# Attention and feed-forward on one core: order of the steps that share a PSUM bank, and the score banks of the first batch's last tiles

## The chip, the cores and the metric

The kernel runs on one core of one Trainium2 chip. The metric is the device time of one execution in microseconds, the median over several runs. TensorE (PE in the views, PEld for its weight loads) multiplies, VectorE (DVE), ScalarE (ACT) and GpSimd (POOL) do the rest, SyncE (SP) issues the transfers.

## The reference

```python
scores = scale * np.matmul(q, k.transpose(0, 1, 3, 2))       # 8 x 8 heads, 576 x 64
thresh = np.max(scores, axis=-1, keepdims=True) - tau
scores = np.where(scores >= thresh, scores, -1000000000.0)
scores = scores - np.max(scores, axis=-1, keepdims=True)
attn = np.exp(scores)
attn = attn / (np.sum(attn, axis=-1, keepdims=True) + 1e-09)
x = np.matmul(attn, v)               # heads joined: 4608 x 512
h = x @ w_in                         # 512 x 2048
r = np.maximum(h, 0.0)
g = s * (r * r) + b
out = g @ w_out                      # 2048 x 512
```

## The kernel before

Attention goes by tiles of 128 queries of one head. The first batch has 36 tiles (`n_plain` = 36), computed with fp32 products (`plain_tile`): scores on TensorE into a PSUM bank, row maximum on DVE (line 529), threshold on POOL (531), exponential on ACT (533), mask and sum on DVE (535), reciprocal (538, 540), scaling on POOL (541), transposes on TensorE (549), copy on ACT (553), products with v (562), copy-out (566). The other seven batches (`split_tile`) work with pairs of fp16 pieces, and their attention is transposed by DMA.

The feed-forward takes blocks of 256 rows. Each has a stage (scaled fp16 pieces of x, lines 806 to 828) and 16 steps: 24 products into bank `h`, relu, square and cast on ACT (847, 850, 851), a remainder (852), and 24 products into the double bank `o`. At the end, line 871 scales `o` and adds a row that comes from `b`. Three pairs of buffers `gs` (tiles `gh`, `gl`) pass from the h products to the o products.

The weights arrive in 16 parts (f = 0 to 15) and are decoded (lines 670, 673, 665). `weight_sizes(k)` for four parts at a time takes products into bank `h` and their maximum (688, 692). `sums(k)` adds the columns of four parts of w_out: eight product records into bank `h` (768), copied (772) or added (774) into `part`; after k = 3 a product with `both` spreads the sum over the partitions (777) and ACT multiplies it with `b` (778). `bias` later copies it to its place (781). `weight_scales` reduces the maxima (698), turns them with a product into bank `h` (701), reduces (702), spreads (706) and makes the power `wpower` (707 to 715). `pieces_of_weights(f)` needs `wpower` and splits every part in two fp16 pieces, first on ACT (737), then on DVE (741).

`keep_busy` adds filler products (983) without use for the result. All steps are added to a plan with engine, cost, what they read and write, and a due time. The order in which they are added decides which of two steps that write the same buffer or bank comes first. `Plan.run` then lists the steps of each engine by a cost model, and `NUDGES` shifts the due time of chosen steps (kind, number, how many, by how many ns) before the last listing. The order of events is that of the number in front of each. Tiles with i < `TWO_BANKS` use score bank `s` or `o` in turn, later plain tiles all use `s`.

Of the kernel before, what the change touches and what calls it, by code (L numbers as in the profile page):

```python
# [23 lines left out]


NUDGES = (
# [35 lines left out]
)  # L62


# [2 lines left out]
LEAST, UP, DOWN = 2.0 ** -120, 2.0 ** -52, 2.0 ** 51  # L67
H_DOWN = 2.0 ** -21
BUSY, BUSY_TILES, BUSY_EACH = 16, 12, 5
TWO_BANKS = 30  # L70
WEIGHTS_AT, WEIGHTS_EACH = 12, 1.5
STACKS_IN = (None, 0, 7, 8, 9, 10, 11, 12)
VALUES_IN = (1, 2, 3, 4, 5, 6)
SPARES = (2, 3, 1, 5, 6, 4)


# [119 lines left out]
def tile_attention_ffn(ctx: ExitStack, tc: tile.TileContext, qT, kT, v, tau, w_in, w_out, s, b, out):  # L196
# [65 lines left out]
    def spare(f):  # L262

        return lazy["whole", SPARES[f], 0]

# [19 lines left out]
    def split_buffers():  # L285
# [9 lines left out]
        for n, f in enumerate(STACKS_IN):  # L295
# [4 lines left out]
            claim([f"y{n}"] + (old_ if f is None else [(f"w{f}", "o")]) + [("y", n, c) for c in range(2)], y)  # L300
        for n, f in enumerate(VALUES_IN):
            def y(n=n, f=f):
# [477 lines left out]
    def bias(at):  # L780
        act((465, 565), lambda: nc.scalar.copy(out=spare(2), in_=part),
            ["part", (f"w{SPARES[2]}", "i", 2)], ["bias"] + [f"g{n}{i}" for n in "hl" for i in range(3)], at)

# [182 lines left out]
    n_plain = sum(vis[0] == 0 for vis in visits) // 2 * 9  # L966
# [46 lines left out]
    events = []  # L1013
# [15 lines left out]
    for f in range(NF):  # L1029
        events.append((WEIGHTS_EACH * f, lambda f=f: (load_weights(f, 2 + f), weights(f, 2 + WEIGHTS_EACH * f))))  # L1030
        if f % 4 == 3:
            events.append((WEIGHTS_EACH * f + 0.1, lambda f=f: (weight_sizes(f // 4, 2.5 + WEIGHTS_EACH * f), sums(f // 4, 2.5 + WEIGHTS_EACH * f))))
    events.append((n_plain - 0.6, lambda: weight_scales(WEIGHTS_AT)))
    for f in range(NF):
        events.append((n_plain - 0.5, lambda f=f: convert(f)))
    events.append((n_plain - 0.4, lambda: bias(WEIGHTS_AT + 2)))
    step, when = 0, 0.0
    for i, ti in enumerate(tiles):
        ti.tag = "o" if i < TWO_BANKS and i % 2 else "s"

# [68 lines left out]
```

## Time and profile before

| | us |
|---|---|
| median of 3 runs | 1121.05 |
| lowest, highest | 1116.58, 1124.85 |
| profiled execution, its own time | 1119.29 |
| span of the profiled execution | 1117.4 |
| PE busy | 1093.1 |
| ACT busy | 965.8 |
| DVE busy | 914.1 |
| POOL busy | 541.0 |

The profile holds one execution. Busy time is the time in which at least one instruction of an engine is under way; for TensorE, products overlap and their ends are modelled. The granted TensorE clock is 0.998 of full speed.

### The profile page before, as it was taken

The numbers are of one execution on the slowest core, as the hardware profiler recorded it, in microseconds if no ns is written. First come the engines' busy times: TensorE is split into PE (matmuls) and PEld (weight loads), VectorE is DVE, ScalarE is ACT, GpSimd is POOL, SyncE is SP. The second block draws the span as 40 slices with busy tenths as digits, with TensorE's granted clock in tenths as the row PEclk, the third lists the DMA queues.
The fourth block names the chain that finished last, engine by engine and source line by source line (L and its number), as shares of the span: only waits on it lengthen the run. The fifth ranks groups of instructions, "written<-read, shape, count | busy, mean of one in ns | idle before, by whom it ended". The sixth has DMA issues, their size and how long they took to land.

```text
span 1117.4 us, 38384 instructions
## 1 busy us (share of the span) xinstructions
PE 1093.1 (98%) x15026; PEld 948.0 (85%) x15026; DVE 914.1 (82%) x1947; ACT 965.8 (86%) x2293; POOL 541.0 (48%) x1113
## 2 busy tenths in 40 slices
PE   9999999999999999999999999999999999999998
PEld 7776777878788999888999998888888988888876
DVE  6897888999899999989988899988989888884021
ACT  8996988899899989999988899989989989995443
POOL 6645554455446445555544455545535455553200
PEclk9999999999999999999999999999999999999999
DMA  9920079879986998879876789868887976472000
GB/s 286 393 95 1 14 163 198 123 149 170 185 158 122 186 190 169 150 141 186 175 133 104 145 153 184 150 120 174 149 147 144 173 134 146 89 127 45 10 21 21
DMA packets 359078, 157.05 MB, mean 141 GB/s; under 512 B 313328, under 2 KB 340464, under 8 KB 358896
## 3 DMA queue, kind: packets, MB, share of 16 engines
q1 hardware_dynamic: 358896, 154.60, 69.5%
q8 instruction: 118, 1.93, 0.7%
q14 instruction: 64, 0.52, 0.1%
HBM read 46.01 MB, written 9.44 MB: 50 GB/s over the span
## 4 chain that ended last, share of the span: by engine, by line
PE 74%; ACT 8%; DMA 7%; DVE 7%; issue 3%; POOL 0%; SPq 0%; DVEq 0%; ACTq 0%; POOLq 0%
PE h L277 26%; PE o L277 26%; PE pv L626 7%; DMA eb<-en 4%; PE t L277 4%; PE s L277 3%; DMA ea<-en 2%; ACT en L608 2%; PE s L526 2%; PE pv L562 2%; PE t L549 1%; DVE em L602 1%; ACT em L600 1%; PE o L526 1%; DVE st L594 1%
## 5 line engine op out<-in xcount | busy, mean ns | idle before, releaser
L277 PE MATMUL h<-xp,iw 128*64 128x256 f16 x6912 | 438.5, 273 | 6.9 <-ACT iw L847 6.7
L277 PEld LDWEIGHTS <-iw 128*64 128x64 f16 x6912 | 399.1, 110 | 32.0 <-issue 11.2
L277 PEld LDWEIGHTS <-gs 128*64 128x64 f16 x3456 | 251.0, 110 | 67.8 <-POOL gs L852 1.6
L852 POOL TENSOR_TENSOR gs<-iw,gs 128x256 f16<-128x256 f32 x272 | 198.1, 729 | 198.9 <-ACT gs L851 92.4
L277 PE MATMUL o<-ow,gs 128*64 128x512 f16 x1944 | 251.9, 380 | 0.5 <-POOL gs L852 0.5
L611 DVE SCALAR_TENSOR_TENSOR en<-em,st,en 128x576 f16<-128x576 f32 x252 | 208.6, 830 | 20.8 <-ACT en L608 19.0
L608 ACT ACTIVATE en<-em,st 128x576 f16<-128x576 f32 x252 | 193.5, 770 | 18.3 <-DMA eb<-en 7.6
L277 PE MATMUL o<-iw,gs 128*64 128x512 f16 x1512 | 195.7, 379 | 0.2 <-DVE iw L871 0.2
L596 POOL TENSOR_SCALAR st<-st,wz 128x1 f32<-128x1 f32 x252 | 122.8, 488 | 109.5 <-DVE st L594 67.2
L847 ACT ACTIVATE iw<-h 128x256 f32<-128x256 f32 x288 | 108.9, 378 | 66.6 <-PE h L277 63.0
L605 POOL TENSOR_SCALAR st<-st 128x1 f32<-128x1 f32 x252 | 88.1, 350 | 137.5 <-DVE em L602 71.9
L850 ACT ACTIVATE iw<-iw 128x256 f32<-128x256 f32 x288 | 120.0, 417 | 3.5
L851 ACT CAST gs<-iw 128x256 f16<-128x256 f32 x288 | 116.0, 403 | 5.3 <-PE o L277 1.6
L277 PEld LDWEIGHTS <-ow 128*64 128x64 f16 x1568 | 104.4, 110 | 17.6 <-issue 5.1
L602 DVE SCALAR_TENSOR_TENSOR em<-t,st,em 128x576 f32<-128x576 f32 x126 | 102.1, 811 | 11.1 <-ACT em L600 6.7
L602 DVE SCALAR_TENSOR_TENSOR em<-s,st,em 128x576 f32<-128x576 f32 x126 | 102.0, 809 | 9.3 <-ACT em L600 7.6
L600 ACT ACTIVATE em<-t,st,wz 128x576 f32<-128x576 f32 x126 | 104.1, 826 | 1.5 <-DVE en L611 0.6
L594 DVE TENSOR_REDUCE st<-s 128x1 f32<-128x576 f32 x126 | 94.3, 749 | 13.4 <-PE s L277 11.5
L600 ACT ACTIVATE em<-s,st,wz 128x576 f32<-128x576 f32 x126 | 103.9, 825 | 1.3 <-DVE en L611 0.4
L594 DVE TENSOR_REDUCE st<-t 128x1 f32<-128x576 f32 x126 | 94.3, 749 | 8.7 <-PE t L277 6.5
L598 ACT ACTIVATE st<-st,wz 128x1 f32<-128x1 f32 x252 | 73.0, 290 | 24.7 <-DVE st L594 24.2
L626 PE MATMUL pv<-eb,ow 128*64 128x256 f16 (+1 forms) x588 | 78.9, 286 | 3.3 <-DMA eb<-en 3.2
(188 smaller groups left out, 1603.7 us busy)
## 6 DMA issues: line engine op xcount, KB each, us to landing
ow<-k SPq DMA_DIRECT2D x98, 216.0 KB, 4.0
rk<-in_k_dram SPq DMA_DIRECT2D x29, 288.0 KB, 3.8
ow<-in_moe_w_out_dram SPq DMA_DIRECT2D x16, 512.0 KB, 8.7
iw<-in_moe_w_in_dram SPq DMA_DIRECT2D x16, 512.0 KB, 8.8
out_dram<-iw SPq DMA_DIRECT2D x32, 256.0 KB, 3.0
rq<-in_q_dram SPq DMA_DIRECT2D x28, 288.0 KB, 4.1
rv<-in_v_dram SPq DMA_DIRECT2D x56, 128.0 KB, 3.1
qs<-k SPq DMA_DIRECT2D x14, 216.0 KB, 3.6
```

Source lines behind the costliest of these rows:

```text
L277: nc.tensor.matmul(out[own], stat[:, own], moving, start=start, stop=stop)
L594: dve((667, 750), lambda: nc.vector.tensor_reduce(out=top, in_=ps, axis=mybir.AxisListType.XY, op=ALU.max, negate=True), [bk], [(ks_, 0)], ...
L596: pool((290, 255), lambda: nc.gpsimd.tensor_scalar(out=line, in0=top, scalar1=-1.0, scalar2=va.wz[:, 2:3], op0=ALU.mult, op1=ALU.add), [(k ...
L600: act((716, 885), lambda: nc.scalar.activation(out=halves, in_=ps, func=AF.Exp, bias=bias, scale=va.wz[:, 1:2]), [bk, (ks_, 4), (va.kwz, 1 ...
L602: dve((738, 820), lambda: nc.vector.scalar_tensor_tensor(out=halves, in0=ps, scalar=line, in1=halves, op0=ALU.is_ge, op1=ALU.mult, accum_o ...
L608: act((666, 760), lambda: nc.scalar.activation(out=pieces[:, 0:S], in_=ex, func=AF.Copy, scale=unit), [em_k, (ks_, 3)], [en_k], i)
L611: dve2((728, 830), lambda: nc.vector.scalar_tensor_tensor(out=pieces[:, S + T:2 * S + T], in0=ex, scalar=unit, in1=pieces[:, 0:S], op0=ALU ...
L626: nc.tensor.matmul(ps[j * D:(j + 1) * D], hd.values()[:, (n + 1) % 5, u * D:(u + 1) * D], lazy[("ea", "eb")[j]][:, n, g.c0:g.c0 + g.n], st ...
L847: act((264, 400), lambda: nc.scalar.activation(out=g(), in_=ps, func=AF.Relu, scale=H_DOWN), [h, (f"w{SPARES[(0, 1, 5)[k3]]}", "i", 2)], [ ...
L850: act((307, 430), lambda: nc.scalar.activation(out=g(), in_=g(), func=AF.Square), [kg], [kg], at)
L851: act((295, 405), lambda: nc.scalar.copy(out=hi, in_=g()), [kg], [f"gh{k3}"], at)
L852: do((735, 735) if not self.last else (400, 490), lambda: eng.tensor_tensor(out=lo, in0=g(), in1=hi, op=ALU.subtract), [kg, f"gh{k3}"], [f ...
```

## The change

Three things are changed. `TWO_BANKS` goes from 30 to 36, so that all plain tiles use the two score banks in turn. `sums(2)` and `sums(3)`, with the product and the copy-out that follow the latter, are added to the plan after `weight_scales` and no longer right after the sizes of their four parts. The table of nudges is a new one: 277 entries before, 151 after, 13 of them the same.

```diff
 NUDGES = (
-    (21, 184, 81, -5135), (48, 240, 18, -4130), (62, 85, 13, 1398), (56, 164, 88, -491), (40, 33, 6, -1430), (49, 54, 2, 3633), (55, 137, 56, 4172), (20, 84, 14, 1415),
...
+    (31, 1, 2, -4118), (48, 240, 18, -4130), (55, 66, 103, -9422), (62, 43, 1, -13875), (22, 263, 25, -1546), (67, 30, 21, 8967), (20, 84, 14, 1415), (56, 174, 78, -12338),
...
 )
...
 BUSY, BUSY_TILES, BUSY_EACH = 16, 12, 5
-TWO_BANKS = 30
+TWO_BANKS = 36
 WEIGHTS_AT, WEIGHTS_EACH = 12, 1.5
 STACKS_IN = (None, 0, 7, 8, 9, 10, 11, 12)
 VALUES_IN = (1, 2, 3, 4, 5, 6)
+SUMS_LATE = (2, 3)
...
         if f % 4 == 3:
-            events.append((WEIGHTS_EACH * f + 0.1, lambda f=f: (weight_sizes(f // 4, 2.5 + WEIGHTS_EACH * f), sums(f // 4, 2.5 + WEIGHTS_EACH * f))))
+            events.append((WEIGHTS_EACH * f + 0.1, lambda f=f: (weight_sizes(f // 4, 2.5 + WEIGHTS_EACH * f), f // 4 in SUMS_LATE or sums(f // 4, 2.5 + WEIGHTS_EACH * f))))
     events.append((n_plain - 0.6, lambda: weight_scales(WEIGHTS_AT)))
+    for k in SUMS_LATE:
+        events.append((n_plain - 0.55, lambda k=k: sums(k, WEIGHTS_AT + 0.5)))
     for f in range(NF):
         events.append((n_plain - 0.5, lambda f=f: convert(f)))
```

## Rows read from the trace of the kernel before

**Rows 1.** The page, busy us of each engine (share of the span) and instructions.

```profile
PE 1093.1 (98%) x15026; PEld 948.0 (85%) x15026; DVE 914.1 (82%) x1947; ACT 965.8 (86%) x2293; POOL 541.0 (48%) x1113
```

**Rows 2.** Busy time by stage: stretch, its us, PE, PEld, DVE, ACT, POOL, PEclk, DMA, GB/s.

```profile
94.60:104.00 9.40, 8.62 (x77) 5.71 (x77) 5.95 (x20) 3.90 (x8) 3.67 (x10) 1.00 0.01 2
...
110.00:130.00 20.00, 19.04 (x261) 14.94 (x261) 17.08 (x28) 20.00 (x45) 9.98 (x12) 1.00 0.02 3
...
150.00:300.00 150.00, 140.62 (x1967) 116.91 (x1964) 136.86 (x295) 133.72 (x327) 76.51 (x158) 0.99 0.92 167
300.00:425.00 125.00, 122.16 (x1773) 112.11 (x1770) 117.50 (x254) 115.94 (x284) 66.13 (x137) 1.00 0.87 161
425.00:1050.00 625.00, 623.04 (x8996) 556.38 (x8993) 526.81 (x1119) 557.49 (x1368) 309.22 (x633) 1.00 0.74 139
```

**Rows 3.** Chain of waits that ended last, 1080 to 1118 us: start, us, what.

```profile
1103.96 1.29 PE o L277 x12
1105.25 1.31 PE h L277 x24
```

**Rows 4.** Busy time by stage in tens of microseconds, 70 to 110 us.

```profile
70.00:80.00 10.00, 10.00 (x91) 7.07 (x89) 9.63 (x20) 9.96 (x19) 5.36 (x10) 1.00 0.01 2
...
90.00:100.00 10.00, 9.55 (x58) 5.70 (x57) 7.25 (x15) 5.87 (x9) 6.48 (x14) 1.00 0.00 0
100.00:110.00 10.00, 8.86 (x101) 6.79 (x100) 6.90 (x17) 7.64 (x14) 4.56 (x14) 1.00 0.01 2
```

**Rows 5.** Users of tile wpower: ns min/median/max, first and last start in us.

```profile
L737 ACT ACTIVATE iw<-iw,wpower x16: 707/786/819, 104.0 to 136.4; 128x512 f16<-128x512 f32 x16
```

**Rows 6.** Chain of waits (first row), then timeline: the steps on bank h.

```profile
74.83 1.72 PE h L768 x8
...
89.68 0.16 DVE L698 TENSOR_REDUCE wnorm<-wmost 128x2 f32<-128x8 f32 x1
...
92.43 1.94 PE L768 MATMUL h<-ow,ones 128*64 128x512 f32 x8
...
94.80 0.69 DVE L774 TENSOR_TENSOR gs<-h,gs 128x512 f32<-128x512 f32 x1
...
97.64 0.68 ACT L778 ACTIVATE gs<-h,b_t 128x512 f32<-128x512 f32 x1
...
99.89 0.38 PE L701 MATMUL h<-eb,wnorm 128*2 128x128 f32 x2
...
100.68 0.27 DVE L702 TENSOR_REDUCE wnorm<-h 2x1 f32<-2x128 f32 x1
...
104.01 0.72 ACT L737 ACTIVATE iw<-iw,wpower 128x512 f16<-128x512 f32 x1 [1.14 <-POOL wpower L715]
```

**Rows 7.** Score products: one line's first and last, then timeline of tiles 29 to 35.

```profile
L526 PE MATMUL s<-rk,rq x24: 406/406/510, 6.1 to 62.4; 128*128 128x288 f32 x16, 128*64 128x288 f32 x8
...
89.85 1.14 PE L526 MATMUL s<-k 128*128 128x288 f32 x4
90.82 1.13 PE L526 MATMUL o<-k 128*128 128x288 f32 x4
...
114.24 1.24 PE L526 MATMUL s<-ea 128*128 128x288 f32 x4
...
119.30 0.80 DVE L535 SCALAR_TENSOR_TENSOR em<-s,st,em 128x576 f32<-128x576 f32 x1
```

**Rows 8.** Timeline of TensorE: the feed-forward's first h and first o products.

```profile
107.27 1.48 PE L277 MATMUL h<-xp,iw 128*64 128x256 f16 x24
...
118.55 0.84 PE L277 MATMUL o<-iw,gs 128*64 128x512 f16 x6
```

**Rows 9.** Line 541, a tile's scaling on POOL, 90 to 110, then 110 to 130.

```profile
L541 POOL TENSOR_SCALAR em<-em,st x6: 739/740/744, 89.9 to 104.1; 128x576 f32<-128x576 f32 x6
...
L541 POOL TENSOR_SCALAR em<-em,st x3: 799/1103/1675, 112.6 to 122.6; 128x576 f32<-128x576 f32 x3
```

**Rows 10.** Chain of waits, 150 to 300 us: the longest of seven transposing DMAs.

```profile
282.50 7.63 DMA eb<-en
```

52 rows, old and new, of the table NUDGES are left out of this document.

## The prediction

> **What bounds the kernel now.** I read the engines' busy times first. TensorE (PE) is busy in 98% of the span, more than any other engine [rows 1]. That is an average over stages, so the second view is the busy time by stage. From 425 to 1050 us TensorE is busy 623.04 of 625 us; from 300 to 425 it lacks 2.84 us, from 150 to 300 it lacks 9.38 [rows 2]. In the feed-forward tail the chain of waits alternates 1.31 us of h products and 1.29 us of o products without a break [rows 3]. A change that removes no matmul can gain only where TensorE idles, and from 425 to 1050 us that is 1.96 us.
>
> So the stage to look at is the first one. The view by stage, in tens of microseconds, shows ScalarE (ACT) busy 9.96 of 10 from 70 to 80 us, then 5.87 and 7.64 between 90 and 110 [rows 4], then 20.00 of 20 until 130 [rows 2]. VectorE (DVE) is at 9.63 before and at 7.25 and 6.90 in the two slices between [rows 4]. This is a lull between two stages limited by ACT: the decoding of the weights before, their splitting into fp16 pieces (32 on ACT and 32 on DVE; the row of 16 of ACT's is in [rows 5]) after. TensorE looks busy in it, but a good part is latency of single products: only 77 matmuls start in the 9.4 us from 94.6 to 104.0, against 261 in the 20 us that follow [rows 2].
>
> Two things make the lull. First, the pieces wait for the weights' power, and its only full-width step, the product of line 701, uses PSUM bank h. Everything else it needs is ready when wnorm is reduced at 89.68 to 89.84, but in program order the last sums over columns come first on that bank: sums(3) 92.43 to 94.37, its add to 95.49, then the product with `both` and its copy-out to 98.32, and only then line 701 at 99.89 [rows 6]. Second, tiles 30 to 35 all use score bank s: their six score products start from 89.85 to 114.24, 4.9 us apart [rows 7], each waiting for the mask (line 535) of the one before. Tiles 0 to 29, in two banks, start between 6.1 and 90.82, 2.9 us apart (84.7/29) [rows 7].
>
> **The change part by part.**
>
> *Weights' powers first.* From line 701 (99.89) to the first piece on ACT (104.01) the chain takes 4.1 us [rows 6]. Started at 90.0 it gives the first piece at 94.1; I allow 0.5 us for TensorE's queue and take 94.6, 9.4 us earlier. What that buys is not 9.4, because ACT must still do all its work. Between 94.6 and 104.0 ACT is busy 3.90 us [rows 2], so 5.5 us of it are free for pieces (seven at 0.79). From 110 to 130 ACT is full, and its pieces run past 136 [rows 2, 5], so 5.5 us taken out ahead end that stage 5.5 us earlier. Bounds: 0, if the pieces in the lull only wait for something else, and 9.4, if the whole stage shifts with its first piece. The nearest row is ACT's free time, so I take **-5.5**.
>
> *The last two sums later.* Nothing is added: 8 products of 1.94 us each time and an add of 0.69 on DVE [rows 6] are moved. sums(2) leaves 74.83, where DVE is at 9.63 of 10 [rows 4, 6]: its add there is worth at most 0.7, **-0.7**. What the move may cost is bank h. After line 702 has read it (1.06 us after line 701 starts, so about 91.1), two sums of 3.06 us (92.43 to 95.49) and 2.8 us of final product and copy-out (95.49 to 98.32) stand before the first h product: 91.1 + 6.1 + 2.8 = 100.0. Before, the first h product came at 107.27 [rows 8], so even behind both sums it is 7.3 us earlier; the first step also needs the first piece on ACT and DVE, which it followed by 3.3 us (107.27 - 104.01), so 97.9, earlier still. The cover is thus 7.3 us; without it the sums would cost their 6.1 us. No DMA is issued or moved past a queue by this: the DMA share is at 0.00 to 0.01 in these slices [rows 4].
>
> *Two score banks until tile 35.* Three tiles go to bank o. At the old pace for two banks the last score product would start near 91 + 5 x 2.9 = 105.5 instead of 114.24. This makes no work vanish; it only keeps ACT and DVE fed in the lull, and it is what lets the first term be reached. I add **0** for it (bounds: 0, and -8.7 if the tiles and not ACT ended the stage, which the full ACT from 110 to 130 excludes). Its price: the first o product of the feed-forward (118.55, [rows 8]) must now wait for the mask of tile 35, at 119.30 to 120.1 before [rows 7]. If that tile didn't come earlier, o would start at 120.1, +1.6, with three steps of room in the gs buffers.
>
> *Port.* Pieces and plain tiles now overlap for six tiles instead of three. In the trace the scaling of a tile (line 541, POOL) takes 739 to 744 ns between 90 and 110, with few pieces about, and 799, 1103 and 1675 from 110 to 130, beside the pieces of line 741 [rows 9]. Three more tiles at 1103 - 740 = 0.36 us: **+1.1**, bounds 0 and +2.8 (at 1675). The Trainium skill's page SBUF — State Buffer, section "Who interferes with whom", says that a VectorE instruction with two SBUF inputs and a GpSimd instruction that reads SBUF shut each other out for a whole instruction, and line 741 has two such inputs. That rule speaks against this change: if every one of the six tiles met a piece as the slowest did (1675 - 740 = 0.94 us), the term would be +5.6 and the sum -0.6. The rows above agree in direction, and the sum stays with them.
>
> *The table of nudges.* 277 entries are replaced by 151, 13 of them the same. They shift due times and so the order on every engine over the whole run. No row prices this. From above the gain is bounded by TensorE's idle time between 150 and 1050: 9.38 + 2.84 + 1.96 = 14.2 [rows 2]; from below by as much again if holes of the same size open. Both tables fit their own list of steps, and most of the run is within 0.5% of full, so I take **0**.
>
> Sum: -5.5 - 0.7 + 0 + 1.1 + 0 = -5.1. On the profiled execution (1119.3, span 1117.4) that is 1114.2. This execution stands 1.8 below the median of the runs (1121.05); on the median it is 1116.0. I say **1115**. It arrives at the end undiminished only if TensorE's later stretch simply starts earlier: it has little slack from 300 on, so it can give the lead back only in the holes of 150 to 300.
>
> **The rivals.**
>
> *The lead is given back (no change).* Between 150 and 300 the chain runs over seven transposing DMAs, the longest of 7.63 us [rows 10]. If what releases them does not move, the holes there grow by what the lull lost. For it: TensorE misses most here. Against it: these DMAs come after tiles that wait for the pieces and the last plain tiles on the same ACT queue. Time 1119 to 1121, and 1125 if the port takes its worst (+5.6) besides.
>
> *More is filled (faster by over 1%).* A lead in the feed-forward is also stock for TensorE in the holes of 150 to 425 (12.2 us). If two thirds of it go besides, -5.1 - 8.1 = -13.2: about 1107. For it: the new table orders just this stretch anew. Against: those holes wait for attention's transposes.
>
> *The new order doesn't build the stock (slower).* TensorE is full after 300 only because the feed-forward lags behind attention. Its idle share from 150 to 300 is 9.38/150 = 6.3%. If the new table leaves it there past 300, each 100 us costs 6.3 less what is idle there now. It decides from 11.2 us net, some 230 us longer (14.4 - 3.2), with the lull's gain used up: 1133. For it: the smaller table rests on no row. Against: nothing in the code touches a dependency after tile 36.
>
> *Pages by which another number would come.* By busy weight loads TensorE would not be the limit: they are at 85% [rows 1]. Against that stands the unbroken alternation in the tail [rows 3]: 2.60 us a step with no gap is all it can do, so no gain follows from it. The Trainium skill's page Perfetto Trace Analysis, section "Identifying the Most-Contended Engine", calls matmul busy time a poor measure and weight loads a better one; by it there would be 15% of headroom and -13 us would not be the end of rival two. I leave that in its chance.
>
> **How the numbers follow.** A measurement of this kernel tells about 1% (11.2 us) from no change: faster is below 1109.8, slower above 1132.3. Forecast, the lull filled in part (1110 to 1119): 0.48. Lead given back or eaten by the port (1119 to 1126): 0.17. More filled (below 1110): 0.23. Slower (above 1132): 0.12. So faster 0.23, same 0.65, slower 0.12. The range 1104 to 1126 leaves out the slow case and the end of the fast one, 0.06; 0.82 lie in it. Alone, the forecast's range is 1110 to 1119: the sum with its bounds of -9.4 and 0.
>
> **What would show it.** Right: line 701 starts near 90, the first piece (line 737) near 95 and the first h product near 100, with both sums between; ACT near full from 95 on; the score products of tiles 30 to 35 some 3 us apart, alternating s and o; first o product before 112; the last piece near 131; TensorE from 300 on as full as before, the lead kept to the end. Wrong: line 701 late all the same; line 541 and 741 both well over 1 us through six tiles; bank o free only at 120; more than 9.4 us idle on TensorE between 150 and 300, or more than 3 between 300 and 600.

## The result, and the profile after

The changed kernel takes 1109.49 us (median; 1107.49 to 1109.99), the kernel before took 1120.2 in the same job. The ratio is 0.9899, 95% interval 0.9859 to 0.9938. A second job with more runs gave 1108.71 against 1118.7, ratio 0.9907 (0.9887 to 0.9926). By these ratios the gain is 10.4 to 11.3 us; forecast were 5.1 us, and 1115 on the median. The direction held and the time lies in the range of 1104 to 1126. It lies just below the bracket that the forecast alone was given (1110 to 1119), and the size is twice the sum.

Line numbers after are 15 lower than before (L594 is now L579, L277 is L262). In the kernels with a written-out order (below) they are 167 higher than before, so that L277 is L444 and L594 is L761. The page's first part, as in [rows 1]:

```profile
PE 1089.3 (98%) x15026; PEld 932.9 (84%) x15026; DVE 916.4 (83%) x1947; ACT 961.5 (87%) x2293; POOL 542.3 (49%) x1113
```

Nothing was taken away from TensorE: the same 15026 products, and still 98%. Busy time by stage, in the stretches of [rows 2] and the columns named there (PE, PEld, DVE, ACT, POOL, clock, DMA, GB/s):

```profile
94.60:104.00 9.40, 9.40 (x84) 6.36 (x83) 7.67 (x19) 7.76 (x15) 6.15 (x18) 1.00 0.01 2
110.00:130.00 20.00, 19.40 (x284) 16.32 (x285) 17.96 (x28) 20.00 (x46) 9.06 (x12) 1.00 0.07 18
...
150.00:300.00 150.00, 147.45 (x2109) 127.92 (x2106) 142.41 (x307) 139.43 (x341) 80.29 (x163) 1.00 0.90 177
300.00:425.00 125.00, 122.80 (x1777) 106.01 (x1774) 117.13 (x253) 115.36 (x289) 65.93 (x135) 1.00 0.87 160
425.00:1050.00 625.00, 623.36 (x8998) 545.04 (x8995) 520.42 (x1104) 549.98 (x1354) 306.38 (x628) 1.00 0.74 136
```

Two rows moved. In the lull ACT went from 3.90 to 7.76 us busy and DVE from 5.95 to 7.67. And from 150 to 300 us TensorE's idle time went from 9.38 to 2.55 us: 6.8 us, more than the lull was thought to give. Behind 300 us the idle time is nearly what it was (2.84 and 1.96 before, 2.20 and 1.64 after).

Busy time counts the latency of single products as work, so the number of products says more about TensorE's progress. It stands in brackets behind the busy time. In the first 150 us, before and after:

```profile
0.00:150.00 150.00, 144.76 (x1467) 112.10 (x1469) 121.92 (x260) 130.94 (x249) 84.43 (x179) 1.00 0.48 158
0.00:150.00 150.00, 142.52 (x1442) 110.96 (x1444) 125.50 (x267) 132.65 (x252) 86.97 (x183) 0.99 0.49 160
```

By 150 us the changed kernel has started 25 products fewer, and TensorE's idle time has grown from 5.24 to 7.48 us. The feed-forward is behind by 27 h products (and 6 o products), while attention's second form is ahead by 8:

```profile
L277 PE MATMUL h<-xp,iw 128*64 128x256 f16 x343 | 21.6, 273 | 0.0
L262 PE MATMUL h<-xp,iw 128*64 128x256 f16 x316 | 19.7, 273 | 0.2 <-ACT iw L832 0.2
```

From 150 to 300 us it starts 142 products more (2109 against 1967). At the pace of 425 to 1050 us, 14.4 products per us, that is an estimated 10 us. So the early part gives TensorE no lead of its own: nearly the whole gain is made from 150 to 300 us.

Where the early part ends can be read from the first row maximum of a split tile. The line's users in the kernel before (ns min/median/max, first and last start):

```profile
L594 DVE TENSOR_REDUCE st<-s x126: 730/750/759, 149.9 to 1000.9; 128x1 f32<-128x576 f32 x126
```

and after:

```profile
L579 DVE TENSOR_REDUCE st<-s x126: 731/750/759, 144.5 to 992.6; 128x1 f32<-128x576 f32 x126
```

Attention's second form starts 5.4 us earlier, and its last row maximum on bank s is 8.3 us earlier. In a second profile of the changed kernel, of the slowest run in the second job (1112.75 us), the two are 5.1 and 5.3 us earlier (144.8 and 995.6), so a lead that grows on the way is not the rule.

The steps on bank h in the changed kernel, from the timeline (start, us, engine, line), to be set beside [rows 6] and [rows 8]:

```profile
90.33 0.38 PE L686 MATMUL h<-eb,wnorm 128*2 128x128 f32 x2
92.48 1.89 PE L753 MATMUL h<-ow,ones 128*64 128x512 f32 x8
...
92.81 0.21 DVE L689 TENSOR_SCALAR wtop<-eb,wnorm 2x2 f32<-2x2 f32 x1
...
95.88 0.28 PE L691 MATMUL pv<-wtop,ones 128*128 128x2 f32 x2
...
97.62 1.33 ACT L722 ACTIVATE iw<-iw,wpower 128x512 f16<-128x512 f32 x2
...
100.07 1.94 PE L753 MATMUL h<-ow,ones 128*64 128x512 f32 x8
...
104.34 1.13 PE L762 MATMUL h<-gs,both 128*128 128x512 f32 x2
...
110.83 0.74 ACT L763 ACTIVATE gs<-h,b_t 128x512 f32<-128x512 f32 x1
...
111.63 1.50 PE L262 MATMUL h<-xp,iw 128*64 128x256 f16 x24
...
120.39 0.84 PE L262 MATMUL o<-iw,gs 128*64 128x512 f16 x6
```

The product that turns the maxima (L686) starts at 90.33 instead of 99.89, the first piece (L722) at 97.62 instead of 104.01. But the first h product of the feed-forward starts at 111.63, 4.4 us later than before, and the first o product 1.8 us later. The gain is thus not a feed-forward that begins earlier.

### The profile page after: what moved, and what is told of

It reads as the page before. It is cut to its first block, busy times and chain, and to the rows that moved or that the text cites. A ratio compares the mean times of both kernels' runs of the same rounds, so it can differ in the third digit from the quotient of the medians.

```text
span 1108.0 us, 38433 instructions
## 1 busy us (share of the span) xinstructions
PE 1089.3 (98%) x15026; PEld 932.9 (84%) x15026; DVE 916.4 (83%) x1947; ACT 961.5 (87%) x2293; POOL 542.3 (49%) x1113
## 4 chain that ended last, share of the span: by engine, by line
PE 68%; ACT 6%; DMA 4%; DVE 2%; issue 2%; DVEq 0%; SPq 0%; POOL 0%; ACTq 0%
PE h L262 26%; PE o L262 26%; PE pv L611 7%; PE s L262 4%; PE t L262 4%; DMA eb<-en 2%; DMA ea<-en 2%; ACT en L593 2%; ACT em L585 1%; DVE em L587 1%; ACT iw L832 1%; PE t L574 1%; DMA rv<-in_v_dram 0%; DVE en L596 0%; ACT st L583 0%
## 5 line engine op out<-in xcount | busy, mean ns | idle before, releaser
L262 PE MATMUL h<-xp,iw 128*64 128x256 f16 x6912 | 434.9, 273 | 2.8 <-ACT iw L832 2.3
L262 PEld LDWEIGHTS <-iw 128*64 128x64 f16 x6912 | 393.4, 110 | 30.7 <-issue 6.7
L262 PEld LDWEIGHTS <-gs 128*64 128x64 f16 x3456 | 239.5, 110 | 77.6 <-POOL gs L837 0.6
L837 POOL TENSOR_TENSOR gs<-iw,gs 128x256 f16<-128x256 f32 x272 | 201.1, 740 | 193.0 <-ACT gs L836 75.1
L262 PE MATMUL o<-ow,gs 128*64 128x512 f16 x1944 | 246.3, 379 | 0.1
L262 PE MATMUL o<-iw,gs 128*64 128x512 f16 x1512 | 195.6, 379 | 0.2 <-DVE iw L856 0.2
L262 PEld LDWEIGHTS <-ow 128*64 128x64 f16 x1568 | 101.5, 110 | 15.3 <-issue 3.0
L579 DVE TENSOR_REDUCE st<-s 128x1 f32<-128x576 f32 x126 | 94.5, 750 | 12.6 <-PE s L262 10.2
L579 DVE TENSOR_REDUCE st<-t 128x1 f32<-128x576 f32 x126 | 94.5, 750 | 9.3 <-PE t L262 5.9
```

The lines of the kernel that those rows point to most:

```text
L262: nc.tensor.matmul(out[own], stat[:, own], moving, start=start, stop=stop)
L579: dve((667, 750), lambda: nc.vector.tensor_reduce(out=top, in_=ps, axis=mybir.AxisListType.XY, op=ALU.max, negate=True), [bk], [(ks_, 0)], ...
L837: do((735, 735) if not self.last else (400, 490), lambda: eng.tensor_tensor(out=lo, in0=g(), in1=hi, op=ALU.subtract), [kg, f"gh{k3}"], [f ...
```

## The experiments

The theory after the first look: the early order fills the lull (5 us at the first split tile), and something behind it closes the holes from 150 to 300 us. That can be the lead itself, or the new order of the steps there, which the table of nudges and the planner made. The rivals: all of it is the lead; all of it is the order behind.

**Both halves crossed at the first split tile.** The order of all steps is written out from the two kernels, so that nothing is planned anew. `ORDER` lists the steps of one kernel until the first row maximum of a split tile, and all that remain in the order of the other. For the first of the two, banks and sums are those of the kernel before:

```diff
-TWO_BANKS = 36
+TWO_BANKS = 30
-SUMS_LATE = (2, 3)
+SUMS_LATE = ()
...
-        return [ops[n][3] for _, n in self.order]
+        return [ops[n][3] for n in ORDER]
```

> Same steps as both kernels, with the order of every engine written out: that of the kernel before (its banks, its sums first) until the first row maximum of a split tile, from there the order of the changed kernel. Theory A (the lull gave about half, the new order behind it the other half): the first split row maximum stays at 149.9 us as before, the second half of the gain is there, about 1115 (ratio 0.995 to 0.997). Rival B (all of the gain is the lead of the early part): 1120, ratio 1.00, with the TensorE idle time between 150 and 300 us back at some 9 us. Rival C (all of it is the order behind): 1110, ratio 0.990.

Measured: 1115.5 us, ratio 0.9971 (0.9956 to 0.9986), about -3 us. The other half has only the last two lines of the diff:

> The other half: order and banks of the changed kernel until the first row maximum of a split tile, from there the order of the kernel before. Theory A: first split row maximum at 144.5 us as in the changed kernel, lead of 5 us kept to the end and nothing more, about 1115 (0.995). Rival B: 1110 (0.990). Rival C: 1120 (1.00).

Measured: 1118.25 us, ratio 0.9981 (0.9963 to 0.9998), about -2 us. Neither rival holds. Theory A holds for h1 but not for h2, where 1115 was expected, and the halves do not add up to the whole: 3 and 2 against 10 to 11. The busy time by stage shows why. First h1 (early part of before, order of after behind it; its first row maximum of a split tile is at 151.3 us):

```profile
150.00:160.00 10.00, 6.03 (x74) 4.82 (x71) 7.61 (x17) 6.48 (x14) 3.97 (x10) 0.89 0.54 154
150.00:300.00 150.00, 144.08 (x2036) 124.51 (x2033) 141.65 (x306) 138.60 (x335) 80.63 (x165) 0.99 0.90 175
```

Of its 5.92 us of idle time, 3.97 lie in the first ten microseconds; the other 140 us hold 1.95, as few as in the changed kernel. TensorE's waits from 150 to 160 us name the cause (engine, line, waited for: us, times, longest), a score product that waits for the mask of a tile that comes too late:

```profile
PE s L444 <- DVE em L769: 3.5, 1, 3.5
```

So the new order has few holes behind 160 us, but it counts on attention being further ahead (144.5 us instead of 151.3). Without that lead TensorE stands until the mask is there. Now h2 (early part of after, order of before behind it), its first split tile and its stages:

```profile
L761 DVE TENSOR_REDUCE st<-s x126: 730/750/759, 142.3 to 1002.3; 128x1 f32<-128x576 f32 x126
```

```profile
150.00:300.00 150.00, 142.00 (x2016) 118.22 (x2013) 139.24 (x302) 135.68 (x332) 77.32 (x161) 1.00 0.92 169
300.00:425.00 125.00, 122.00 (x1768) 109.59 (x1766) 117.88 (x250) 116.42 (x285) 65.23 (x136) 1.00 0.87 164
425.00:1050.00 625.00, 619.12 (x8908) 547.21 (x8906) 522.96 (x1112) 552.53 (x1356) 304.06 (x628) 1.00 0.75 137
```

It has a lead of 7.6 us at 142.3, and still 8.00 us of idle time from 150 to 300, nearly the 9.38 of before, and 5.88 from 425 to 1050 where before had 1.96. The waits of 150 to 300 us tell what these holes are: TensorE's wait for ACT's read of bank h, and ACT's own waits for the transposing DMAs. In the kernel before:

```profile
PE h L277 <- ACT iw L847: 5.7, 4, 2.5
...
ACT en L608 <- DMA eb<-en: 6.7, 5, 3.0
ACT en L608 <- DMA ea<-en: 2.8, 3, 1.1
```

in h2:

```profile
PE h L444 <- ACT iw L1014: 4.1, 4, 1.8
...
ACT en L775 <- DMA eb<-en: 6.6, 4, 2.3
...
ACT en L775 <- DMA ea<-en: 1.1, 2, 0.7
```

and in the changed kernel:

```profile
PE h L262 <- ACT iw L832: 0.5, 2, 0.2
...
ACT en L593 <- DMA ea<-en: 2.1, 2, 1.3
...
ACT en L593 <- DMA eb<-en: 1.0, 1, 1.0
```

Most of the holes, 5.7 of 9.38 us before, are h products whose half of bank h ACT has not yet read. ACT's queue has other work ahead of the ReLU, and some of that work waits itself. Just ahead of the longest hole (2.47 us, until 292.37) ACT stands for the DMA of [rows 10], in a step of attention that its queue has before the ReLU:

```profile
290.22 0.77 ACT L608 ACTIVATE en<-em,st 128x576 f16<-128x576 f32 x1 [3.00 <-DMA eb<-en]
```

These waits of ACT add up to 9.5 us before, 7.7 in h2 and 3.1 in the changed kernel. So an earlier start alone leaves most of the idle time, as h2 shows; another order of the two queues, with the lead that it needs, removes it. h2 is not without gain there (it starts 49 products more than the kernel before from 150 to 300 us), but it gives it back from 425 to 1050 us, as the table of products further down shows.

**The two parts of the change, each alone.** The same splice, with the changed kernel's order behind the first split tile, and before it an order planned for one part alone, with the new table. For the two banks:

```diff
-SUMS_LATE = (2, 3)
+SUMS_LATE = ()
...
-        return [ops[n][3] for _, n in self.order]
+        return [ops[n][3] for n in ORDER]
```

> The changed kernel with the two banks for tiles 30 to 35 but the last sums where they were, until the first row maximum of a split tile; from there the order of the changed kernel. Theory A (each part alone leaves the lull): weights' power at 103 to 104 us as before, the plain tiles' last score product some 5 us earlier, first split row maximum at 147 to 150, so 3 to 5 us over the changed kernel, about 1113 to 1115 (0.994 to 0.997). Rival: the banks carry it alone, 1110 (0.990).

Measured: 1118.55 us, ratio 0.9992 (0.9973 to 1.001). For the sums alone:

```diff
-TWO_BANKS = 36
+TWO_BANKS = 30
...
-        return [ops[n][3] for _, n in self.order]
+        return [ops[n][3] for n in ORDER]
```

> The same with the last sums behind the weights' power but one score bank for tiles 30 to 35. Theory A: first piece near 97 us, tiles still 4 to 5 us apart, first split row maximum at 147 to 152, 1113 to 1116 (0.994 to 0.997). Rival: the order of the sums carries it alone, 1110 (0.990).

Measured: 1118.73 us, ratio 0.9991 (0.9977 to 1.0005). Both lose all of the gain, more than was expected. The first split tile with two banks alone:

```profile
L761 DVE TENSOR_REDUCE st<-s x126: 729/751/758, 152.0 to 1003.3; 128x1 f32<-128x576 f32 x126
```

and with the sums alone:

```profile
L761 DVE TENSOR_REDUCE st<-s x126: 729/751/759, 153.2 to 1001.5; 128x1 f32<-128x576 f32 x126
```

At 152.0 and 153.2 it is later than in the kernel before (149.9). That the new table does not fit either early part is the likely reason, which no run shows by itself; this pair speaks of the parts and of the table at once. The next four kernels leave the table out.

**Without any table.** Planned anew with an empty table, in four forms:

```diff
-NUDGES = (
...
-)
+NUDGES = ()
```

> The kernel before with an empty table of nudges: 5 to 15 us over 1120 if the table mattered, 1120 if not.

> The changed kernel with an empty table of nudges, to be compared with nn_before. Theory A: some 5 us below nn_before, as the sum for the banks and the order of the sums has it. Rival D (the banks and the sums give something only with a table fitted to them): within 2 us of nn_before. How far both lie above 1120 says what a table is worth: between 5 and 15 us are expected.

> Empty table of nudges, two banks alone; nn_before was 1134.6, nn_after 1125.3. Theory A: between them, 1128 to 1134. Rival: as nn_after, 1125.

> Empty table of nudges, late sums alone. Theory A: between nn_before and nn_after or as nn_before, 1130 to 1136: the pieces come early but the plain tiles stay in one bank, and the sums stand in front of the first h product. Rival: as nn_after, 1125.

| | median us | ratio to the kernel before | interval |
|---|---|---|---|
| nn_before | 1134.56 | 1.0132 | 1.0111 to 1.0153 |
| nn_two | 1129.35 | 1.0090 | 1.0073 to 1.0107 |
| nn_sums | 1131.9 | 1.0109 | 1.0093 to 1.0126 |
| nn_after | 1125.3 | 1.0051 | 1.0033 to 1.0068 |

Two banks alone give 0.42 points (4.7 us), the late sums alone 0.23 (2.6 us), both 0.81 (9.1 us). The interval of nn_sums overlaps those of nn_before and of nn_two, so that the sums gain by themselves, and less than the banks, is likely but not clear of the noise. Rival D falls: the banks and the sums together give their gain without a fitted table. And a table is worth 1.32 points before (from nn_before to the kernel before) and 1.44 to 1.52 after (from 1.0051 to 0.9907 or 0.9899): the two tables are equal within some 2 us, which is inside the intervals.

Where the 9.1 us lie in this pair is only partly settled. TensorE's stretch from 150 to 300 us in nn_before:

```profile
150.00:300.00 150.00, 141.85 (x2004) 119.74 (x2002) 138.31 (x301) 134.59 (x330) 77.44 (x160) 1.00 0.88 171
```

and in nn_after:

```profile
150.00:300.00 150.00, 142.54 (x2043) 122.97 (x2041) 141.42 (x305) 138.30 (x337) 78.56 (x163) 1.00 0.91 175
```

differ by 0.7 us only in busy time, but by 39 products. The two profiled executions are 5.9 us apart in span (1130.6 and 1124.7), less than the medians. By products, nn_after is 51 ahead at 300 us and 78 at 1050, an estimated 3.5 and 5.4 us. Attention's start does not follow the total: the first row maximum of a split tile is at 152.1 us in nn_before, 149.1 in nn_two, 149.5 in nn_after, and 157.4 in nn_sums, which is not slower than nn_before for it.

**Both orders crossed at 300 us.** `ORDER` again, now cut at the ReLU of feed-forward step 50 (some 283 us in the changed kernel), with the unchanged kernel after beside it:

> The changed kernel again, in the same job as the two that follow and in more runs: 1109 to 1110 (0.990), so that the parts can be set against the whole.

> Order and banks of the changed kernel until the ReLU of feed-forward step 50 (some 283 us), from there the order of the kernel before. Theory A' (the gain is made in the first 300 us, where the order is planned on attention's lead, and TensorE is full behind it under any order): the lead of 7 to 8 us at 300 us stays, 1112 to 1113 (0.993). Rival (an order loses what it was not planned on, as the seam of h1 lost 5 us): 1116 or more (0.997).

> The mirror: the kernel before until step 50, from there the order of the changed kernel. Theory A': 1119 to 1121 (1.00), since nothing is gained before 300 us and little can be behind. Rival (the new table's order behind 300 us gains by itself): 1116 or less.

Measured: 1108.71 (0.9907) for the changed kernel; 1110.97 us, ratio 0.9937 (0.9915 to 0.9958), with its order until 300 us alone; 1121.09 us, ratio 1.0024 (1.0011 to 1.0037), with its order behind 300 us alone. So 7.0 of the 10.4 us of this job are made by the order until 300 us (4.7 to 9.5 by the interval), and the order behind 300 us gains nothing by itself, it loses 2.7. Theory A' holds in its number; its reason, that any order would do behind 300 us, does not quite, since behind the first part of the kernel before the new order is slower, clear of the noise. That the last 3.4 us come only where the changed kernel's own order follows its own first part is not shown: the two intervals overlap.

The products of TensorE that have been started by a time, set against the kernel before (1467, 3429 and 14188), place each gain and loss. Each row is one profiled execution (that of h6 its slowest run, 1116.1 us); 14 products are about 1 us.

| | by 150 us | by 300 us | by 1050 us |
|---|---|---|---|
| changed kernel | -25 | +117 | +124 |
| changed kernel, second profile | -25 | +109 | +82 |
| h1 | -19 | +49 | +46 |
| h2 | +22 | +71 | -19 |
| h6 | +5 | +90 | +44 |
| h7 | -1 | +9 | -32 |

Every kernel that is ahead at 300 us has won most or all of it from 150 to 300 us. At 300 us the two halves nearly add up to the whole, 49 products of h1 and 71 of h2 against 109 to 117; what is missing from their times was lost behind it. h2 and h6, where the order of the kernel before follows, lose 90 and 46 products behind 300 us. The changed kernel's two executions differ there too, by 34.

**A hole near 10 us.** In the changed kernel's profile the slices from 5 us on read:

```profile
5.00:10.00 5.00, 3.67 (x18) 2.69 (x18) 1.52 (x2) 3.18 (x6) 1.11 (x3) 1.00 0.99 233
10.00:15.00 5.00, 3.22 (x8) 2.36 (x9) 2.55 (x7) 1.32 (x3) 2.98 (x8) 0.66 1.06 315
```

A granted clock of 0.66 is a mean of the two levels, 1.2 and 2.4 GHz. TensorE had stood 2.83 us before it, and the next four score products took 2.29 us instead of 1.24:

```profile
5.28 1.24 PE L511 MATMUL s<-rk,rq 128*128 128x288 f32 x4 [0.32 <-POOL rq L384]
...
11.78 2.29 PE L511 MATMUL s<-rk,rq 128*128 128x288 f32 x4 [2.83 <-DVE em L520]
```

That it stood does not decide it alone: with the same early order, h2 stood 2.08 us there and kept a clock of 1.00, h6 stood 1.90 us and fell to 0.69. Ten filler products ahead of this place were issued three times:

```diff
+            def fill(at=len(fillers)):
+                for _ in range(3 if 16 <= at < 26 else 1):
+                    nc.tensor.matmul(bank["pv"][:, P:P + NB], ones, qt[:, 0:NB], start=True, stop=True)
+            fillers.append(0)
-            whole_pe(1, 2 * P, lambda: nc.tensor.matmul(bank["pv"][:, P:P + NB], ones, qt[:, 0:NB],
-                                                 start=True, stop=True), ["ones", "qt0"] + r, ["idle"], 1e6)
+            whole_pe(1, 2 * P, fill, ["ones", "qt0"] + r, ["idle"], 1e6)
```

> The changed kernel in its own order, with ten of the filler products behind the first two score products issued three times instead of once. In the changed kernel's profile TensorE stood 2.83 us there, its granted clock was 0.66 from 10 to 15 us, and the plain tiles were 3.6 us late at tile 10; the same order in h2 had clock 1.00 and 1.5 us. If that clock costs the kernel its time: 1107 to 1108 and fewer high runs; if the lost 2 us are made good later or the runs seldom show them: 1109 to 1111.

Measured: 1112.87 us, ratio 0.9954 (0.9937 to 0.9972): 4 us slower than the changed kernel in the same job, against both expectations. The fillers did their part. Slice and first split tile of this kernel:

```profile
10.00:15.00 5.00, 5.00 (x36) 4.58 (x35) 3.72 (x9) 2.40 (x4) 3.68 (x10) 1.00 1.05 344
```

```profile
L761 DVE TENSOR_REDUCE st<-s x126: 730/750/759, 142.9 to 998.3; 128x1 f32<-128x576 f32 x126
```

The clock is 1.00 and attention starts 1.6 us earlier than in the changed kernel (142.9 against 144.5; h2, with the same clock and no fillers added, 142.3), but its last row maximum on bank s is 5.7 us later (998.3 against 992.6; 995.6 in the second profile). The time went behind 425 us. The stage in this kernel and in the second profile of the changed one, and the wait in this kernel:

```profile
425.00:1050.00 625.00, 619.14 (x8909) 552.14 (x8906) 519.50 (x1102) 548.48 (x1348) 302.70 (x626) 1.00 0.75 136
425.00:1050.00 625.00, 621.64 (x8958) 536.74 (x8956) 521.20 (x1104) 549.36 (x1352) 304.57 (x627) 1.00 0.73 136
```

```profile
PE pv L793 <- DMA eb<-en: 3.4, 5, 1.5
```

5.86 us are idle, 3.4 of them waits for transposing DMAs. The changed kernel has 1.64 and 3.36 us idle there in its two profiles, with 0.2 us and none of that wait on TensorE. Without the 20 extra products this kernel is 118 products ahead of the kernel before at 300 us, as the changed kernel is, and only 42 at 1050 us. Both compared profiles are of slower runs (1115.65 and 1112.75 us). That an order which fits its own timing this closely loses by a shift of less than 2 us is the likely reading; no run moved the timing without adding products.

## Why the prediction was right or wrong, point by point

**The bound.** Right. Nothing was gained from 300 us on by the new order itself (h7), and the idle time from 425 to 1050 went only from 1.96 to 1.64. That weight loads at 85% mean headroom found no support: they are at 84% with the same products, and the gain came out of TensorE's holes.

**Weights' powers first.** The mechanism was right, line 701 moved from 99.89 to 90.33 (90.0 was said). The first piece came at 97.62, not 94.6: the chain took 7.3 us instead of 4.1. I had measured it in a lull and moved it into a fuller place. On DVE L689 stood behind a row maximum and a mask until 92.81, on TensorE L691 stood behind sums(2), which the change itself had put there, transposes and a score product until 95.88. The size of the term held on ACT all the same: -5.5 was said, ACT took 3.9 us more work in the lull, the last piece of the row in [rows 5] came at 130.1 instead of 136.4, and attention started 5.4 us earlier. On TensorE it did not arrive as a lead: 25 products fewer by 150 us.

```profile
L722 ACT ACTIVATE iw<-iw,wpower x16: 707/774/850, 97.6 to 130.1; 128x512 f16<-128x512 f32 x16
```

**The last two sums.** Wrong in its cover, at a price that was made good later. The first h product was said to be possible at 100.0 and came at 111.63. I had lined up the steps on bank h at their bare durations; in truth the second sum had its turn at 100.07 and the copy-out (L763) stood in ACT's full queue until 110.83, 5.4 us after its input was there. The "7.3 us of cover" became 4.4 us of delay, and two signs of being right failed with it: a first h product near 100 and a first o product before 112. The 27 h and 6 o products that are missing at 150 us are some 2 us at the pace of [rows 3] (an estimate: 27 x 1.31/24 + 6 x 1.29/12), and by 300 us they are made good. No run moved this step alone in the changed kernel, and none shows the -0.7 for sums(2).

**Two score banks.** The pace was right: the six score products start from 94.90 to 109.80, 3.0 us apart, s and o in turn. Counting it at 0 beside the first term was wrong. Without a table the banks alone give 4.7 us, clear of the noise, and both together 9.1. The two terms cannot be told apart there, since with the banks alone the plan also has the first piece at 100.0 us instead of 106.2.

**The port.** Right in direction and small: +1.1 was said for three more overlapped tiles. Line 541 (now 526) from 104 to 125 us:

```profile
L526 POOL TENSOR_SCALAR em<-em,st x5: 746/1095/1677, 103.2 to 116.5; 128x576 f32<-128x576 f32 x5
```

Five scalings beside the pieces instead of three [rows 9], at the same 1.1 us: 2 x 0.36 = 0.7. The worst case (+5.6, every meeting as long as the slowest), which the prediction set beside the Trainium skill's page SBUF — State Buffer, section "Who interferes with whom", did not come: the median of the five is 0.36 us above 740 ns, half an instruction, and only the slowest is 0.94 us above it.

**The table of nudges.** Counting it at 0 was right as a price of the table: 14.8 us of worth before, 16 to 17 after. It was wrong to take it as separable. Crossed with the other kernel's early part, either order loses 7 to 9 us of the whole.

**What was mis-sized.** The sum of -5.1 is half of the gain, and the step behind it is the last sentence on the sum: that the lead arrives undiminished at best, by TensorE's later stretch simply starting earlier, and can only be given back in the holes from 150 to 300 us. TensorE's later stretch did not start earlier (25 products behind at 150 us). The gain was made in those holes, which shrank by 6.8 us and in which TensorE started 142 products more. So the 5.1 and the 6.8 are not two gains to be added. The lead of attention, and an order in which ACT reads bank h before TensorE wants it again, both work on these holes, and each alone gives a part of TensorE's lead at 300 us: 71 products in h2, 49 in h1, 117 together.

This is the mechanism of the second rival, "more is filled", which stood at 0.23 with two thirds of 12.2 us on top of the lead. That the time lies in the range is thus partly luck: the range was wide enough to hold a rival's mechanism. The forecast's own bracket does not hold it, and as the sum with its bounds (-9.0 and +0.4) that bracket fits the profiled execution; from the median it would be 1112 to 1121. The first rival's transposing DMAs did stand behind the longest of these holes, as the row of ACT at 290.22 shows; the new order waits less for them instead of giving the lead back.

In the pair without tables the hole is hardly smaller, while TensorE starts 39 products more in it. Why the medians there are 9.1 us apart, and the profiled executions only 5.9, stays open.

## What to carry to other kernels

When all queues are planned together, the price of an edit in the first stage is not its own time: take what it frees, and then ask what the stage behind can do with a start that much earlier; holes there that come from two queues out of step can close too. To learn what such an edit is worth, plan both forms without hand-fitted corrections, and splice the two orders at a boundary: a part taken alone, in an order fitted to the whole, shows mostly a misfit. Follow TensorE's progress by its products and not by its busy time, in which the latency of single products counts as work. A chain of small steps timed in a lull takes longer once the lull is filled, here 7.3 us instead of 4.1.

## What the runs showed of the hardware that was not expected

A few microseconds in the first 15 us went with waits 460 to 1000 us later: with 20 filler products more, TensorE waits 3.4 us in all for transposing DMAs from 425 to 1050 us, where the changed kernel's two profiles show 0.2 us and none. Bringing the granted clock from 0.66 to 1.00 for 5 us went with 1.6 us at the first split tile and nothing at the end. The clock fell behind a stand of 2.83 us and of 1.90 us in two executions and did not behind one of 2.08 us in a third, with the same early order.
